# Two heads' last state columns in one matrix product, and the state's increment in two column halves, in an mLSTM cell followed by a gated feed-forward block

## The chip, the core and the metric

The kernel runs on one core of a Trainium2 chip. The metric is the device time of one execution in microseconds (us). The core has a matrix engine (PE, whose weight loads are listed apart as PEld), a vector engine (DVE), an activation engine (ACT), a general engine (POOL), and a queue that starts the transfers (SP). Each works through its own instructions in order and waits on semaphores that the others raise.

## What is computed

An mLSTM cell runs over 768 steps for 4 batch rows and 8 heads of 40 dimensions, and its output goes through a feed-forward block with a cosine gate.

```python
for t in range(S):
    m_new = np.maximum(f_gate[:, :, t] + m, i_gate[:, :, t])
    f_stab = np.exp(f_gate[:, :, t] + m - m_new)
    i_stab = np.exp(i_gate[:, :, t] - m_new)
    m = m_new
    C = f_stab * C + i_stab * np.einsum('bhd,bhe->bhde', vt, kt)
    n = f_stab * n + i_stab * kt
    h_tilde = np.einsum('bhde,bhe->bhd', C, qt)
    denom = np.maximum(np.abs(np.einsum('bhd,bhd->bh', n, qt)[:, :, None]), 1.0)
    y[:, :, t] = sigmoid(o_gate[:, :, t]) * h_tilde / denom
x = y.transpose(0, 2, 1, 3).reshape(3072, 320)
h = x @ w_in            # 320 x 2048
out = (h * np.cos(h)) @ w_out
```

## The kernel before

The 768 steps are cut into 6 chunks `c` of 128. A *cell* `n = 4 * c + b` is one chunk of one batch row with all 8 heads, so there are 24 cells. Inside a cell the recurrence becomes matrix products over 128 steps. Heads 2p and 2p+1 form pair `p`; the key dimensions of the even head lie in partitions 0 to 39, those of the odd head in partitions 64 to 103.

A cell goes through these functions:

- `scores(n)` (L450): keys times queries for each head, the two heads of a pair in the two halves of PE's rows. `weigh(n)` (L456) multiplies by the decay `E`.
- `values(n)`: for n >= 4 the tile `vt` is filled, turned, with 32 output partitions for each of four heads. Four head groups are worked one after another. Each has four products of `vs` (values) with `E` (L474) and four products of the state `st` with the decayed queries (L477), each four on the four 32-column strips of PE. Groups 0 and 1 are dimensions 0 to 31 of heads 0 to 3 and of heads 4 to 7. The third plane `vt[:, 2]` takes the last eight dimensions and the normalizer of all heads. It is filled in two groups: heads 4 to 7 with 32 columns (dimensions 16 to 47, of which only the upper half is kept), then heads 0 to 3 with 16 columns over the lower half.
- `normalize_turned(n)`: DVE divides and gates (L486 to L497), POOL writes two thirds of `xT`, the input of the feed-forward block (L496). `normalize(n)` does this for the first four cells.
- `fade(n)`: POOL multiplies the state by its decay (L529), one operation for each half of the partitions, on 40 partitions by 192 elements.
- `seam(n)`: PE turns the last plane into `px` (L542; for the first four cells L537, and L539 in two 64-column halves), and for n < 20 it computes the state's increment `pu` (L547): one product for each pair of heads, 104 weight columns (both heads' weighed keys) by 96 moving columns (both heads' values). Of this product only the two blocks of a head with itself are used.
- `seam_out(n)`: ACT copies `px` to `xT` (L554). `state(n)` adds `pu` to `st`: two DVE additions of 40 x 192 (L566), or two ACT copies in the first four cells (L564).
- `weigh_k(n)` (POOL, L394) weighs the keys for the increment, and `scale_q(n)` (POOL, L432) decays the queries.

`st[b]` has a place of 48 columns for each head. A head's numbers lie in its own 40 partitions, and the rest of its columns are zero, so a product over all 128 partitions takes one head of the pair.

Every product here is in float32. The trace lists two weight loads and two matmuls for each one, two *passes*, so a count of x8 is four products.

Around the cells runs the feed-forward block, in the hand-written order of `both_parts(c, b)`. It works chunk `c` of the block while cell `n = 4(c+1)+b` is computed. Each cell has two halves, `i = 0` and `i = 1`. PE's order is:

- `i = 0`: up products of this half (`pup`, L583 and L586), `scores(n)`, the down products of the half before (`po`, L615), `values(n)`;
- `i = 1`: up products, `seam(n)`, down products.

In each half ACT rounds the up products (L591), DVE subtracts (L594), ACT takes a sine (L599) and DVE multiplies (L603); in `i = 1` the additions of `state(n)` stand on DVE between L594 and L603. The up products have two buffers, which L603 frees for the next half.

The first four cells are written out by hand in `first_cells`. While cells 4 to 7 run, the weights of the feed-forward block come in as 64-bit floats and are converted piece by piece (`to_float32`, L143 to L151, on ACT, DVE and POOL). All big loads are issued on SP's queue in program order. `load_o(c)` (L300) brings the output gates of a chunk in four transfers, one for each block of 32 partitions; `load_two` (L330, L335) brings queries, keys and values two cells at a time, keys and values only after the `seam` that last read their buffer.

Of the kernel before, what the change touches and what calls it, by code (L numbers as in the profile page):

```python
# [29 lines left out]
def kernel(  # L30
# [63 lines left out]
    nc.gpsimd.affine_select(out=wall, in_=wall, compare_op=OP.is_ge, fill=1.0e30, base=0,  # L94
                            pattern=[[0, HP], [1, C]], channel_multiplier=-1)
    ident_b = const.tile([128, 128], BF, name="ident_b")
    pick = const.tile([128, 2, 2, HP, 8], FP, name="pick")
    for e in range(2):
        nc.gpsimd.tensor_copy(out=pick[:, e], in_=ident.rearrange("q (a g i) -> q g a i", a=HP, g=2)[:, :, :, 0:8])


    DV = 48
# [2 lines left out]
    for i in range(2):  # L105
        nc.gpsimd.memset(ks2[i][:, :, :, D:64], 0.0)
        nc.gpsimd.memset(vs2[i][:, :, :, D:DV], 1.0)

    WR = 2 * HP * (C // 32) * D
# [2 lines left out]
        nc.gpsimd.memset(t[:, WR:WR + 32], 0.0)  # L114


    st = [const.tile([128, H, DV], FP, name=f"st{b}") for b in range(B)]
    for t in st:
        nc.gpsimd.memset(t, 0.0)
    og = const.tile([128, B, 3 * C // 32, 32], FP, name="og")  # L120
# [39 lines left out]

    def weights_in(f):
        for i in range(NK):
            src = [(slice(32 * a, 32 * a + 32), w_in_bits[D * (HP * i + a):D * (HP * i + a) + 32, ts(f, WP)]) for a in range(HP)]
            yield w_in_sb[:, i, ts(f, WP)], bits_in(WP, src, pb, WP)
        src = w_last.rearrange("r (a e n two) -> r e a n two", e=2, n=128, two=2)

        yield (w_in_l[:, ts(f, 2)].rearrange("p a n -> p (a n)"),
               bits_in(256, [(slice(64 * e, 64 * e + 64), src[:, e, ts(f, 2)]) for e in range(2)], pb, WP))
# [119 lines left out]
    def vs(n):  # L288
        return vs2[n // 2 % 2][:, n % 2]

    def load_o(c, bs=range(B)):
        if c == 0:
            sig[c] = og.rearrange("q b k i -> q (b k i)")[:, 0:B * DM].rearrange("q (b h d) -> q b h d", b=B, h=H)
            for b in bs:
                nc.sync.dma_start(out=sig[c][:, b], in_=o_gate[b, :, ts(c, C)].rearrange("h t d -> t h d"))
            return
        raw_o[c] = p1.tile([128, B, 2 * C // 32, D], FP, name="o", tag="o")
        src = o_gate.rearrange("b (g a) (c t k) d -> a c t (b g) (k d)", g=2, k=C // 32, t=32)
        for a in range(HP):
            nc.sync.dma_start(out=raw_o[c][32 * a:32 * a + 32].rearrange("t b (g k) d -> t (b g) (k d)", g=2), in_=src[a, c])  # L300

    def sigmoid(c, bs=slice(0, B)):
        if c == 0:
# [87 lines left out]
    def weigh_k(n):  # L391
        if n < N - B:
            kw = p2.tile([128, H, 64], FP, name="kw", tag="kw")
            nc.gpsimd.tensor_tensor(out=kw, in0=ks(n), in1=cols(n, 1, 64), op=OP.mult)  # L394
            kws[n] = kw

    def psum(n):

        return (ps_o, "o") if n < B and n % 2 == 1 else (ps_a, "a")

    def pair(t, p):
        return t[:, 2 * p:2 * p + 2].rearrange("p j d -> p (j d)")[:, 0:PR]
# [27 lines left out]
    def scale_q(n):  # L430
        qG = p1.tile([128, HP, C], FP, name="qG", tag="qG")
        nc.gpsimd.tensor_tensor(out=qG, in0=qkT[n][0], in1=Gs[n], op=OP.mult)  # L432
        Gs[n] = qG
# [24 lines left out]
    def values(n):  # L458
        pool, tag = psum(n)
        E = Es[n]  # L460
        if n < B:
            ph = pool.tile([128, H, D1], FP, name="ph", tag=tag)
            for j in range(2):
                for p in range(HP):
                    h = 2 * p + j
                    nc.tensor.matmul(ph[:, h], E[:, h], vs(n)[:, h, 0:D1], start=True, stop=True)  # L466
            heads_of[n] = ph
            return
        vt = pool.tile([128, 3, C], FP, name="vt", tag=tag)
        state = st[n % B]  # L470
        for i, g, lo, hi in ((0, 0, 0, 32), (1, 1, 0, 32), (2, 1, 16, 48), (2, 0, 32, 48)):
            for a in range(HP):
                h = HP * g + a
                nc.tensor.matmul(vt[32 * a:32 * a + hi - lo, i], vs(n)[:, h, lo:hi], E[:, h], start=True, stop=False)  # L474
            for a in range(HP):
                h = HP * g + a
                nc.tensor.matmul(vt[32 * a:32 * a + hi - lo, i], state[:, h, lo:hi], Gs[n][:, h // 2], start=False, stop=True)  # L477
        heads_of[n] = vt

    FROM0, FROM1 = 8, 24  # L480
# [19 lines left out]
    def normalize(n):  # L500
        c, b = divmod(n, B)
        hs = heads_of[n]
        dn = p2.tile([128, H], FP, name="dn", tag="dn")

        nc.vector.scalar_tensor_tensor(out=dn, in0=hs[:, :, D], scalar=-TWO_PI, in1=least, op0=OP.mult, op1=OP.max)
        nc.vector.scalar_tensor_tensor(out=dn, in0=hs[:, :, D], scalar=TWO_PI, in1=dn, op0=OP.mult, op1=OP.max)
        nc.vector.reciprocal(out=dn, in_=dn)
        y = p1.tile([128, 3 * C], FP, name="y", tag="yt")[:, 0:DM]
        t = p1.tile([128, 3 * C], FP, name="yo", tag="db")[:, 0:DM].rearrange("q (h d) -> q h d", h=H)
        nc.vector.tensor_tensor(out=t, in0=sig[c][:, b], in1=hs[:, :, 0:D], op=OP.mult)  # L510
        for lo, hi, x in ((0, 32, 0), (32, D, KL)):
            nc.vector.tensor_tensor(out=y[:, x:x + H * (hi - lo)].rearrange("q (h d) -> q h d", h=H), in0=t[:, :, lo:hi],
                                    in1=dn.unsqueeze(2).to_broadcast([128, H, hi - lo]), op=OP.mult)
        ys[n] = y

    ys, pus, pxs = {}, {}, {}
# [1 line left out]
    def halves(n):  # L518
        for j in range(2):
            r = slice(64 * j, 64 * j + D)  # L520
            yield j, r, st[n % B].rearrange("q (p j) d -> q p j d", j=2)[r, :, j]

    def fade(n):

        if B <= n < N - B:
            c, b = divmod(n, B)
            for j, r, s in halves(n):
                d = tab[r, c, 3, ts(b, H)].rearrange("p (a j) -> p a j", j=2)[:, :, j]
                nc.gpsimd.tensor_tensor(out=s, in0=s, in1=d.unsqueeze(2).to_broadcast([D, HP, DV]), op=OP.mult)  # L529

    def seam(n):

        pool, tag = psum(n)
        if n < B:
            px = pool.tile([128, NK + 1, C], FP, name="px", tag=tag)
            for i in range(NK):
                nc.tensor.transpose(px[:, i], ys[n][:, ts(i, 128)], ident)  # L537
            for e in range(2):
                nc.tensor.matmul(px[64 * e:64 * e + 64, NK], ys[n][:, KL:DM], ident, start=True, stop=True)  # L539
        else:  # L540
            px = pool.tile([128, C], FP, name="px", tag=tag)
            nc.tensor.matmul(px, pick.rearrange("q e g a i -> q (e g a i)"), ys[n][:, 2], start=True, stop=True)  # L542
        pxs[n] = px
        if n < N - B:
            pu = pool.tile([128, HP, 2, DV], FP, name="pu", tag=tag)
            for p in range(HP):
                nc.tensor.matmul(pu[0:PR, p].rearrange("p j d -> p (j d)"), pair(kws[n], p),  # L547
                                 vs(n)[:, 2 * p:2 * p + 2].rearrange("p j d -> p (j d)"), start=True, stop=True)
            pus[n] = pu

    def seam_out(n):
# [7 lines left out]

    def state(n):  # L560
        if n < N - B:
            for j, r, s in halves(n):
                if n < B:
                    nc.scalar.copy(out=s, in_=pus[n][r, :, j])  # L564
                else:
                    nc.vector.tensor_tensor(out=s, in0=s, in1=pus[n][r, :, j], op=OP.add)  # L566


    gs, po = {}, {}
# [59 lines left out]
    def first_cells():  # L629
# [107 lines left out]
        load_E(B + 2)  # L737
        decay(B)
        weigh_k(B)
        scale_q(B)  # L740
        for f in range(2, NF // 4):
            last_rows(f)
# [14 lines left out]
    def both_parts(c, b):  # L757
# [3 lines left out]
        for i in range(2):  # L761
# [15 lines left out]
            if i == 0:  # L777
                if cell:
                    weigh(n)
                    if n + 1 < N:  # L780
                        decay_exponents(n + 1)
                for e in range(2):
                    up.sin(e)
                    up.gate(e)
                if b == 0 and c + 1 < NC:
                    sigmoid(c + 1)

                if c == 0 and b > 0 and pieces:
                    to_float32(*pieces.pop(0))
                if cell and n + 1 < N and (c > 0 or b > 0):  # L790
                    decay(n + 1)
            else:
                if cell:
                    seam_out(n)
                if pieces:
                    to_float32(*pieces.pop(0))
                if cell:
                    state(n)
                for e in range(2):
                    up.sin(e)  # L800
                    up.gate(e)
                while pieces:
                    to_float32(*pieces.pop(0))
                if cell and n + 1 < N:
                    weigh_k(n + 1)
            if f2 > 0:
                down(c, f2 - 1)
            elif c > 0:
                down(c - 1, NF // 2 - 1)
# [62 lines left out]
```

## Time and profile before

| What | Value |
|---|---|
| time, median of 3 runs | 587.3 us (586.58 to 589.53) |
| span of the profiled execution | 586.8 us |
| mean granted PE clock | 0.968 |
| one cell from 8 to 19, in the chain | 21.95 us |
| one cell from 20 to 23, in the chain | 21.2 us |
| HBM read, written | 54.07 MB, 5.16 MB |

Of the profiled execution the span is listed and no further time; it lies between the fastest run and the median.

The profile lists each engine's busy time, groups of instructions by source line, and the chain of work that ended last: at each step, what released the step, or the instruction before it on its engine. A row of a group gives the busy time of all its instructions, the mean duration of one in ns, and the idle time of the engine just before them. Matmuls overlap in time, so the mean duration of one is longer than what it adds to PE's time; what it adds is read from the chain, where each piece runs to the start of the next.

### The profile page before, as it was taken

The numbers are of one execution on the slowest core, as the hardware profiler recorded it, in microseconds if no ns is written. First come the engines' busy times: TensorE is split into PE (matmuls) and PEld (weight loads), VectorE is DVE, ScalarE is ACT, GpSimd is POOL, SyncE is SP. The second block draws the span as 40 slices with busy tenths as digits, with TensorE's granted clock in tenths as the row PEclk, the third lists the DMA queues.
The fourth block names the chain that finished last, engine by engine and source line by source line (L and its number), as shares of the span: only waits on it lengthen the run. The fifth ranks groups of instructions, "written<-read, shape, count | busy, mean of one in ns | idle before, by whom it ended". The sixth has DMA issues, their size and how long they took to land.

```text
span 586.8 us, 8874 instructions
## 1 busy us (share of the span) xinstructions
PE 562.0 (96%) x3404; PEld 336.7 (57%) x3404; DVE 361.6 (62%) x677; ACT 257.2 (44%) x411; POOL 140.7 (24%) x170
## 2 busy tenths in 40 slices
PE   8997869888999999999999999999999999999997
PEld 5874435454556556556556556566556566555454
DVE  5665997787666666666666666666666575423131
ACT  4857617184264343373343373343374251233222
POOL 6524354343321221221221221221211110000000
PEclk9858979897999999999999999999999999999999
DMA  9999999974814914914824714914910000010001
GB/s 142 226 232 208 229 245 234 202 167 89 153 47 90 167 32 91 153 46 91 155 44 90 143 55 89 173 26 91 153 45 1 1 2 1 0 45 1 0 1 45
DMA packets 125546, 58.76 MB, mean 100 GB/s; under 512 B 61328, under 2 KB 121824, under 8 KB 125504
## 3 DMA queue, kind: packets, MB, share of 16 engines
q1 hardware_dynamic: 125360, 58.00, 51.2%
q8 instruction: 27, 0.44, 0.4%
q0 software_dynamic: 96, 0.18, 0.1%
q14 instruction: 15, 0.12, 0.1%
q10 hardware_dynamic: 48, 0.02, 0.0%
HBM read 54.07 MB, written 5.16 MB: 101 GB/s over the span
## 4 chain that ended last, share of the span: by engine, by line
PE 82%; DMA 9%; DVE 3%; SPq 3%; POOL 2%; issue 1%; ACT 0%; DVEq 0%; ACTq 0%; POOLq 0%
PE po L615 32%; PE pup L583 26%; PE pup L586 8%; PE ps L450 4%; PE vt L474 3%; DMA bits<-in_moe_w_in_dram 3%; PE vt L477 3%; PE pu L547 2%; DMA vs<-in_v_dram 2%; PE ph L466 1%; DMA G<-G_d 1%; PE px L542 1%; DMA kr<-in_k_dram 1%; SPq L335 1%; DMA o<-in_o_gate_dram 1%; DMA qr<-in_q_dram 1%
## 5 line engine op out<-in xcount | busy, mean ns | idle before, releaser
L615 PE MATMUL po<-w_out_sb,g 128*128 128x320 f32 x768 | 222.6, 444 | 1.8 <-POOL w_out_sb L151 1.8
L615 PEld LDWEIGHTS po<-w_out_sb,g 128*128 128x128 f32 x768 | 145.0, 194 | 66.0 <-issue 10.1
L583 PE MATMUL pup<-xT,w_in_sb 128*128 128x512 f32 x384 | 176.7, 603 | 0.8 <-DVE g L603 0.7
L594 DVE SCALAR_TENSOR_TENSOR n<-pup,n 128x512 f32<-128x512 f32 x96 | 61.7, 684 | 159.4 <-ACT n L591 159.4
L591 ACT ACTIVATE n<-pup 128x512 int32<-128x512 f32 x96 | 51.9, 592 | 238.0 <-PE pup L586 237.9
L583 PEld LDWEIGHTS pup<-xT,w_in_sb 128*128 128x128 f32 x384 | 71.7, 192 | 80.2 <-issue 67.9
L599 ACT ACTIVATE n<-n 128x512 f32<-128x512 f32 x96 | 58.8, 630 | 18.6 <-DVE n L594 16.6
L603 DVE SCALAR_TENSOR_TENSOR g<-pup,n 128x512 f32<-128x512 f32 x96 | 61.6, 683 | 1.7
L381 POOL TENSOR_SCALAR_AFFINE_SELECT E<-E 128x1024 f32<-128x1024 f32 x22 | 24.0, 1091 | 133.7 <-DVE E L380 133.7
L586 PE MATMUL pup<-xT,w_in_l 64*128 64x512 f32 x192 | 54.2, 641 | 0.0
L432 POOL TENSOR_TENSOR qG<-t,G 128x512 f32<-128x512 f32 x20 | 25.4, 1271 | 69.6 <-DVE t L423 64.2
L450 PEld LDWEIGHTS ps<-t,t 40*128 40x128 f32 x384 | 26.6, 200 | 21.5 <-issue 21.2
L450 PE MATMUL ps<-t,t 40*128 40x128 f32 x384 | 28.2, 289 | 10.8 <-DVE t L423 10.8
L474 PE MATMUL vt<-E,vs 128*32 128x128 f32 (+1 forms) x640 | 33.7, 283 | 4.3 <-DMA vs<-in_v_dram 4.3
L496 POOL TENSOR_TENSOR xT<-yt,db 128x256 f32<-128x256 f32 x20 | 14.5, 724 | 96.7 <-DVE db L493 96.7
L389 ACT ACTIVATE E<-E 128x1024 f32<-128x1024 f32 x24 | 25.4, 1058 | 26.7 <-POOL E L381 25.4
L586 PEld LDWEIGHTS pup<-xT,w_in_l 64*128 64x128 f32 x192 | 14.4, 184 | 36.4 <-issue 34.9
L477 PE MATMUL vt<-qG,st 128*32 128x128 f32 (+1 forms) x640 | 33.3, 280 | 0.0
L456 DVE TENSOR_TENSOR E<-ps,E 128x512 f32<-128x512 f32 x48 | 30.7, 679 | 2.6 <-PE ps L450 2.6
L389 ACT ACT_TABLE_LOAD x21 | 26.9, 1283 | 0.4
L380 DVE TENSOR_TENSOR E<-E,tab 128x1024 f32<-128x1024 f32 x22 | 26.7, 1214 | 0.0
L474 PEld LDWEIGHTS vt<-E,vs 128*32 128x32 f32 (+1 forms) x640 | 17.9, 109 | 13.1 <-DVE g L603 6.6
(134 smaller groups left out, 518.2 us busy)
## 6 DMA issues: line engine op xcount, KB each, us to landing
E<-M_d SPq DMA_DIRECT2D x10, 1024.0 KB, 6.0
qr<-in_q_dram SPq DMA_DIRECT2D x40, 160.0 KB, 3.8
kr<-in_k_dram SPq DMA_DIRECT2D x40, 160.0 KB, 4.9
G<-G_d SPq DMA_DIRECT2D x20, 256.0 KB, 6.9
bits<-in_moe_w_out_dram SPq DMA_DIRECT2D x8, 640.0 KB, 6.3
bits<-in_moe_w_in_dram SPq DMA_DIRECT2D x32, 128.0 KB, 4.3
out_dram<-o_sb SPq DMA_DIRECT2D x24, 160.0 KB, 1.8
o<-in_o_gate_dram SPq DMA_DIRECT2D x20, 160.0 KB, 6.0
```

What stands on the lines that cost most here:

```text
L389: nc.scalar.activation(out=Es[n], in_=Es[n], func=AF.Exp, scale=-1.0)
L450: nc.tensor.matmul(ps[j][:, p], kT[r, p], qT[r, p], start=True, stop=True)
L456: nc.vector.tensor_tensor(out=w, in0=pss[n][j], in1=w, op=OP.mult)
L474: nc.tensor.matmul(vt[32 * a:32 * a + hi - lo, i], vs(n)[:, h, lo:hi], E[:, h], start=True, stop=False)
L477: nc.tensor.matmul(vt[32 * a:32 * a + hi - lo, i], state[:, h, lo:hi], Gs[n][:, h // 2], start=False, stop=True)
L583: nc.tensor.matmul(pu, w_in_sb[:, i, ts(2 * f2 + e, 128)], x(i), start=(i == 0), stop=False)
L586: nc.tensor.matmul(pu, w_in_l[r, f2], x(NK, r), start=False, stop=True)
L591: nc.scalar.activation(out=self.n[e], in_=self.pu[e], func=AF.Copy, bias=0.25)
L594: nc.vector.scalar_tensor_tensor(out=self.n[e].bitcast(FP), in0=self.pu[e], scalar=0.25, in1=self.n[e], op0=OP.add, op1=OP.subtract)
L599: nc.scalar.activation(out=r, in_=r, func=AF.Sin, scale=TWO_PI_DOWN)
L603: nc.vector.scalar_tensor_tensor(out=g, in0=self.pu[e], scalar=TWO_PI, in1=self.n[e].bitcast(FP), op0=OP.mult, op1=OP.mult)
L615: nc.tensor.matmul(po[c][b], gs[c, f][:, ts(b, C)], w_out_sb[:, f], start=(f == 0), stop=(f == NF - 1))
```

## The change

The heads are dealt anew over the planes: plane 0 takes the even heads' first 32 dimensions, plane 1 the odd heads', and plane 2 the last part of both heads of a pair, side by side. The state tile is laid out to match: 4 x 32 columns of even heads, 4 x 32 of odd heads, 4 x 32 in which each pair has 16 columns of the even and 16 of the odd head. So plane 2 needs one state product for a pair in place of two. Its odd heads' values come from a new tile `vr2` with 16 zero columns ahead, which POOL fills for two cells at a time (`odd_values`). The state's increment is computed head by head, with 40 weight columns by 48 moving columns, the even head in PE's lower 64 columns and the odd one in the upper 64. `fade` and `state` follow the state's two pieces: four operations for a cell in place of two. The rows of `w_in`, the output gates and the order of `y` follow the new dealing; `load_o` has eight transfers in place of four.

```diff
-    pick = const.tile([128, 2, 2, HP, 8], FP, name="pick")
+    pick = const.tile([128, 2, HP, 2, 8], FP, name="pick")
...
+    vr2 = [const.tile([128, 2, HP, 32], FP, name=f"vr{i}") for i in range(2)]
+    for t in vr2:
+        nc.gpsimd.memset(t, 0.0)
...
-    st = [const.tile([128, H, DV], FP, name=f"st{b}") for b in range(B)]
+    st = [const.tile([128, 2 * HP * DV], FP, name=f"st{b}") for b in range(B)]
...
-            src = [(slice(32 * a, 32 * a + 32), w_in_bits[D * (HP * i + a):D * (HP * i + a) + 32, ts(f, WP)]) for a in range(HP)]
+            src = [(slice(32 * a, 32 * a + 32), w_in_bits[D * (NK * a + i):D * (NK * a + i) + 32, ts(f, WP)]) for a in range(HP)]
...
-        src = o_gate.rearrange("b (g a) (c t k) d -> a c t (b g) (k d)", g=2, k=C // 32, t=32)
+        src = o_gate.rearrange("b (a g) (c t k) d -> a g c t b (k d)", g=2, k=C // 32, t=32)
         for a in range(HP):
-            nc.sync.dma_start(out=raw_o[c][32 * a:32 * a + 32].rearrange("t b (g k) d -> t (b g) (k d)", g=2), in_=src[a, c])
+            for g in range(2):
+                dst = raw_o[c][32 * a:32 * a + 32].rearrange("t b (g k) d -> t g b (k d)", g=2)[:, g]
+                nc.sync.dma_start(out=dst, in_=src[a, g, c])
...
+    def odd_values(n):
+        if n % 2 == 0:
+            src = vs2[n // 2 % 2].rearrange("q n (a g) d -> q n a g d", g=2)[:, :, :, 1, 32:DV]
+            nc.gpsimd.tensor_copy(out=vr2[n // 2 % 2][:, :, :, 16:32], in_=src)
...
-        for i, g, lo, hi in ((0, 0, 0, 32), (1, 1, 0, 32), (2, 1, 16, 48), (2, 0, 32, 48)):
+        for i in range(3):
+            if i < 2:
+                for a in range(HP):
+                    h = 2 * a + i
+                    nc.tensor.matmul(vt[32 * a:32 * a + 32, i], vs(n)[:, h, 0:32], E[:, h], start=True, stop=False)
+            else:
+                for a in range(HP):
+                    nc.tensor.matmul(vt[32 * a:32 * a + 32, i], vr2[n // 2 % 2][:, n % 2, a], E[:, 2 * a + 1], start=True, stop=False)
+                for a in range(HP):
+                    nc.tensor.matmul(vt[32 * a:32 * a + 16, i], vs(n)[:, 2 * a, 32:DV], E[:, 2 * a], start=False, stop=False)
             for a in range(HP):
-                h = HP * g + a
-                nc.tensor.matmul(vt[32 * a:32 * a + hi - lo, i], vs(n)[:, h, lo:hi], E[:, h], start=True, stop=False)
-            for a in range(HP):
-                h = HP * g + a
-                nc.tensor.matmul(vt[32 * a:32 * a + hi - lo, i], state[:, h, lo:hi], Gs[n][:, h // 2], start=False, stop=True)
+                nc.tensor.matmul(vt[32 * a:32 * a + 32, i], state[:, ts(HP * i + a, 32)], Gs[n][:, a], start=False, stop=True)
...
     def halves(n):
         for j in range(2):
             r = slice(64 * j, 64 * j + D)
-            yield j, r, st[n % B].rearrange("q (p j) d -> q p j d", j=2)[r, :, j]
+            for lo, hi, x in ((0, 32, HP * 32 * j), (32, DV, H * 32)):
+                s = st[n % B][r, x:x + HP * 32].rearrange("q (p d) -> q p d", p=HP)
+                yield j, r, s if lo == 0 else s[:, :, 16 * j:16 * j + 16], slice(lo, hi)
...
-            pu = pool.tile([128, HP, 2, DV], FP, name="pu", tag=tag)
+            pu = pool.tile([128, HP, DV], FP, name="pu", tag=tag)
             for p in range(HP):
-                nc.tensor.matmul(pu[0:PR, p].rearrange("p j d -> p (j d)"), pair(kws[n], p),
-                                 vs(n)[:, 2 * p:2 * p + 2].rearrange("p j d -> p (j d)"), start=True, stop=True)
+                for j in range(2):
+                    h = 2 * p + j
+                    nc.tensor.matmul(pu[64 * j:64 * j + D, p], kws[n][:, h, 0:D], vs(n)[:, h], start=True, stop=True)
...
     def state(n):
         if n < N - B:
-            for j, r, s in halves(n):
+            for j, r, s, w in halves(n):
                 if n < B:
-                    nc.scalar.copy(out=s, in_=pus[n][r, :, j])
+                    nc.scalar.copy(out=s, in_=pus[n][r, :, w])
                 else:
-                    nc.vector.tensor_tensor(out=s, in0=s, in1=pus[n][r, :, j], op=OP.add)
+                    nc.vector.tensor_tensor(out=s, in0=s, in1=pus[n][r, :, w], op=OP.add)
...
         weigh_k(B)
+        odd_values(B)
         scale_q(B)
...
                     weigh_k(n + 1)
+                    odd_values(n + 1)
```

More of the change, by code (lines that the diff above doesn't have):

```diff
@@ L96 @@
     ident_b = const.tile([128, 128], BF, name="ident_b")
-    pick = const.tile([128, 2, 2, HP, 8], FP, name="pick")
+    pick = const.tile([128, 2, HP, 2, 8], FP, name="pick")
     for e in range(2):
-        nc.gpsimd.tensor_copy(out=pick[:, e], in_=ident.rearrange("q (a g i) -> q g a i", a=HP, g=2)[:, :, :, 0:8])
+        nc.gpsimd.tensor_copy(out=pick[:, e], in_=ident.rearrange("q (a g i) -> q a g i", a=HP, g=2)[:, :, :, 0:8])
     DV = 48
@@ L510, in normalize @@
         nc.vector.tensor_tensor(out=t, in0=sig[c][:, b], in1=hs[:, :, 0:D], op=OP.mult)
-        for lo, hi, x in ((0, 32, 0), (32, D, KL)):
-            nc.vector.tensor_tensor(out=y[:, x:x + H * (hi - lo)].rearrange("q (h d) -> q h d", h=H), in0=t[:, :, lo:hi],
-                                    in1=dn.unsqueeze(2).to_broadcast([128, H, hi - lo]), op=OP.mult)
+        for lo, hi, o in ((0, 32, y[:, 0:KL].rearrange("q (g a d) -> q a g d", g=2, a=HP)),
+                          (32, D, y[:, KL:DM].rearrange("q (a g d) -> q a g d", g=2, a=HP))):
+            nc.vector.tensor_tensor(out=o, in0=t[:, :, lo:hi].rearrange("q (a g) d -> q a g d", g=2),
+                                    in1=dn.rearrange("q (a g) -> q a g", g=2).unsqueeze(3).to_broadcast([128, HP, 2, hi - lo]), op=OP.mult)
         ys[n] = y
@@ L526, in fade @@
             c, b = divmod(n, B)
-            for j, r, s in halves(n):
+            for j, r, s, w in halves(n):
                 d = tab[r, c, 3, ts(b, H)].rearrange("p (a j) -> p a j", j=2)[:, :, j]
-                nc.gpsimd.tensor_tensor(out=s, in0=s, in1=d.unsqueeze(2).to_broadcast([D, HP, DV]), op=OP.mult)
+                nc.gpsimd.tensor_tensor(out=s, in0=s, in1=d.unsqueeze(2).to_broadcast([D, HP, w.stop - w.start]), op=OP.mult)
     def seam(n):
@@ L561, in state @@
         if n < N - B:
-            for j, r, s in halves(n):
+            for j, r, s, w in halves(n):
                 if n < B:
-                    nc.scalar.copy(out=s, in_=pus[n][r, :, j])
+                    nc.scalar.copy(out=s, in_=pus[n][r, :, w])
                 else:
-                    nc.vector.tensor_tensor(out=s, in0=s, in1=pus[n][r, :, j], op=OP.add)
+                    nc.vector.tensor_tensor(out=s, in0=s, in1=pus[n][r, :, w], op=OP.add)
     gs, po = {}, {}
```

## The prediction

> **What bounds the kernel now.** I read the page first (busy times, the slices), then the chain of waits, then the timeline of one cell, then single groups.
>
> ```profile
> PE 562.0 (96%) x3404; PEld 336.7 (57%) x3404; DVE 361.6 (62%) x677; ACT 257.2 (44%) x411; POOL 140.7 (24%) x170
> ...
> PEclk9858979897999999999999999999999999999999
> DMA  9999999974814914914824714914910000010001
> ```
>
> PE is busy for 96%. The slices (14.7 us each) show two stages: in the first nine DMA is full and PE's clock dips; after them the clock stays high and DMA has room. The chain of waits of one cell (start, length, line) in the second stage:
>
> ```profile
> 190.91 0.35 PE vt L474 x8
> 191.26 0.22 PE vt L477 x8
> ...
> 192.57 0.22 PE vt L477 x8
> 192.79 3.63 PE pup L583 x8
> 196.42 1.06 PE pup L586 x4
> 197.48 0.42 PE px L542 x2
> 197.90 0.72 PE pu L547 x8
> 198.62 4.33 PE po L615 x16
> 202.96 3.43 PE pup L583 x8
> 206.39 1.06 PE pup L586 x4
> 207.45 0.89 PE ps L450 x16
> 208.34 4.50 PE po L615 x16
> ```
>
> Every piece is PE, end to end, and the cell takes 21.95 us. From cell 8 on (138 us) the end is set by PE's own pieces; what they gain or lose is gained or lost in full while the other engines keep up. The early stage is different. The stretches below give length, then busy time and count of PE, PEld, DVE, ACT, POOL, then clock, DMA share and GB/s:
>
> ```profile
> 38.00:41.00 3.00, 2.68 (x11) 1.09 (x11) 2.45 (x8) 0.00 (x0) 0.00 (x0) 0.50 1.18 276
> 105.00:118.00 13.00, 10.38 (x75) 6.34 (x77) 9.34 (x12) 2.31 (x4) 5.42 (x4) 0.87 1.16 193
> 126.00:138.00 12.00, 9.27 (x31) 4.66 (x29) 11.70 (x20) 5.55 (x10) 6.43 (x6) 1.00 0.16 27
> 170.85:192.80 21.95, 21.95 (x147) 13.19 (x147) 14.23 (x27) 11.18 (x19) 5.14 (x6) 1.00 0.41 91
> ```
>
> DMA is at or over a full share until the last weights have landed, then DVE (11.70 of 12.00 us) converts them, and only then is PE the bound.
>
> **State products.** `vt` goes from eight groups of four products to seven: the odd heads' values (32 columns), the even heads' (16) and one state product of 32 columns for a pair. A group of x8 costs 0.22 us in the chain whether its weight columns are 32 (191.26) or 16 (192.57), since 128 moving columns pace it. So one group less is 0.22 us for each of the cells 8 to 23: 16 x 0.22 = 3.5 us. For cells 4 to 7 (another 0.9) I take nothing, since PE idles there for data; the 0.9 goes into the range.
>
> **The increment.** No row shows 40 x 48 products in column halves, so I bound them. Four products of 104 x 96 cost 0.72 us, 90 ns a pass. The `ph` products (L466: 128 weight columns, 41 moving) take 1.74 us for x16 in the early chain, 109 ns: the weight load paces these. The slope is 19 ns over 24 columns, 0.79 ns each, and 40 columns come to 90 - 64 x 0.79 = 39 ns. By moving columns: four strips side by side pass 128 columns in 0.22 / 2 = 0.11 us, and `po` passes 320 in 4.33 / 16 = 0.271 us, 0.84 ns a column, which makes 48 columns 0.11 - 80 x 0.84 ns = 42 ns. The longer decides: 42 ns.
>
> Do two halves run side by side? The nearest row has just this form, the 64-column halves of `px` in a first cell:
>
> ```profile
> 26.63 0.22 PE px L537 x2
> 26.85 0.37 PE px L539 x4
> 27.22 0.90 PE pu L547 x8
> ```
>
> Four passes of 128 columns one after another would be 0.44 us; they took 0.37 with what it costs to change between full width and halves. That cost is in the chain: the first group of `vt` 0.35 against 0.22 (0.13 to go in); `pu` 0.90 after the halves against 0.72 after a full-width piece, and `po` 4.50 after the row halves of `ps` against 4.33 (0.17 to 0.18 to come out). In `seam` the old `pu` had neither. New: 8 x 0.042 + 0.13 + 0.17 = 0.64 us, against 0.72, a gain of 0.08. With no overlap at all: 16 x 0.042 + 0.30 = 0.97, a loss of 0.25. I take the overlap, by its nearest row L539. Cells 8 to 19: 12 x 0.08 = 1.0 us gained; at the other end 3.0 lost.
>
> The Trainium skill speaks against this part: "TensorEngine Tiling (Array Packing)", section "Instruction Overhead", states some 60 cycles of overhead for each matmul, so that one free column lasts as long as 60, and advises against a tiling factor out of a dimension that is already small. The shortest products of the trace (41 moving columns, `ph`) are paced by their weight loads, so no row shows this. By the rule 48 columns would cost as 60 do, an estimate of 42 + 12 x 0.84 = 52 ns, `pu` would be 0.72, and the gain of this part nothing: 1.0 us less in the sum.
>
> **DVE's four additions.** The groups that show it:
>
> ```profile
> L486 DVE TENSOR_SCALAR dt<-vt 128x128 f32<-128x128 f32 x20 | 5.9, 293 | 24.2 <-PE vt L477 24.2
> L566 DVE TENSOR_TENSOR st<-st,pu 40x192 f32<-40x192 f32 x32 | 11.1, 347 | 0.5
> L529 POOL TENSOR_TENSOR st<-st,tab 40x192 f32<-40x192 f32 x32 | 17.2, 538 | 1.2
> ```
>
> From 192 elements (347 ns) and 128 (293) the slope is 0.84 ns; 128 and 64 elements come to 293 + 239 = 532 ns against 347, twice a cell: 0.37 us more, and at most 0.69 if a piece costs what the whole did. Queued behind are the two gates L603, which PE's next up products wait for. In the timeline:
>
> ```profile
> 243.29 0.72 DVE L566 TENSOR_TENSOR st<-st,pu 40x192 f32<-40x192 f32 x2
> 244.04 1.29 DVE L603 SCALAR_TENSOR_TENSOR g<-pup,n 128x512 f32<-128x512 f32 x2
> ...
> 246.68 3.60 PE L583 MATMUL pup<-xT,w_in_sb 128*128 128x512 f32 x8
> ```
>
> The gates end at 245.33 and PE needs their buffers at 246.68, so 1.35 us of `po` cover the 0.37. A shorter `pu` moves PE and DVE's start alike. In `i = 0` PE comes 0.22 earlier against a cover of 1.7 (gates to 256.81, up products at 258.54). Nothing in cells 8 to 19. In cell 7 DVE is on the chain (state at 129.28, gates, L583 idle 0.33 for the gate, then the transposes that `ps` waits 2.62 for): +0.37 there.
>
> **POOL, SP, ACT, `normalize`.** `fade` goes to four operations. From 192 elements (538) and 256 (L496, 724) up to 512 (1055 for L394) a piece of 128 is near 440 and one of 64 near 330: +0.46 us a cell, done by 241.6, against the addition at 243.29; uncovered it would be 12 x 0.46 = 5.5. `odd_values` is a copy of 128 elements, between 236 ns (L99, 64 elements) and 540, each second cell; behind it on POOL stand `scale_q` (246.43) and the mask L381, after idle times of 4.15 and 8 us. For cell 4 it waits for `vs`, with `scale_q(4)` behind it at 54.78, just when `vs` has landed: +0.3, in the stage that DMA sets. `load_o` adds four issues of 0.46 us (L300's median): 1.8 us of SP ahead of `bits`, `ks` and `vs` at 43.4 to 51.9. DMA is over full just then, so queued transfers cover them; later `load_o`s have idle SP behind them (121.8 to 137.2). Two `vr2` memsets of 256 elements, some 0.3 us each, stand in POOL's opening chain (0.6). Against these in the first cells, `pu` follows halves already, and four increments fall from 0.90 to 1.64 us to about 0.5 to 0.9, 2 us less of PE, and ACT's copies grow by 0.3 us a cell beside it. Until 138 us, after DMA and DVE, I take +0.3 in all, with ends of -2.9 (2 us of `pu`, 0.9 of `vt`) and +3.9 (1.8 SP, 0.6 POOL, 1.5 DVE over cells 4 to 7). The rewritten `normalize` and `w_in` rows keep their counts and sizes: nothing.
>
> **The sum.** -3.5 (state products) - 1.0 (increment) + 0.3 (until 138 us) = -4.2 us on a span of 586.8. The span lies 0.5 under the median, so I carry the change over: 587.3 - 4.2 = 583.1 us.
>
> **Rivals.**
> - *The halves do not overlap.* `pu` 0.97: +3.0 in place of -1.0, so 587.3 - 3.5 + 3.0 + 0.3 = 587.1. For it: no product this small in the trace, and twice the passes. Against it: L539, and the four strips of `vt`.
> - *Each small pass costs what a big one does, one after another* (the side of slower). Place: L547. 16 x 90 ns + 0.30 = 1.74 us, +1.02 for each of 12 cells, 12.2 us, so 587.3 - 3.5 + 12.2 + 0.3 = 596.3. It turns slower than before where `pu` costs over 0.72 + 3.2 / 12 = 0.99 us. Against it: the pace follows the columns in all rows (90 at 104, 109 at 128).
> - *The early stage takes it back.* The 3.9 us above in place of 0.3: 586.7. For it: PE idle 4.33 us for `vs` at 55.97, SP hardly idle, and the clock, which the stretch 138 to 145 shows at 0.52 after PE idled. Against it: DMA is full, and these engines wait for it.
> - *The early stage gains too.* -2.9 in place of 0.3: 587.3 - 3.5 - 1.0 - 2.9 = 579.9.
>
> **How the numbers follow.** A change under 0.5% (2.9 us) can't be told from none here. The forecast has 0.53, with its own range of 581.5 to 584.8: 0.49 of it is faster and 0.04 within. The early gain 0.11 (faster), no overlap 0.13 and the early loss 0.16 (both within), the costly passes 0.07 (slower). So faster 0.60, same 0.33, slower 0.07. The range runs from 580.2 to 587.7: it leaves out the costly passes and most of the early gain.
>
> **What would show it.** The chain of a late cell should have seven groups of `vt` with 1.66 us in place of 1.88, `pu` near 0.64 for x16 with `po` after it at 4.50, and the two at 21.65 us for the cell (was 21.95). L566 should be x64 with a mean near 265 ns, and L583 no wait for L603. `pu` over 0.99, or a wait of PE for DVE or POOL after 150 us, would make me wrong; cell 8's `ps` (138.23) coming later than 139 would show the early loss.

## The result, and the profile after

The changed kernel takes 584.48 us (median of 17 runs, 580.64 to 586.71); the kernel before, in runs beside it, 587.91 us (585.36 to 591.43). The ratio is 0.993, with a 95% interval of 0.9909 to 0.9952: 4.1 us less by the ratio (3.4 by the two medians), uncertain by 1.3, against 4.2 predicted. The profiled execution has a span of 582.6 us and took 584.48, so 1.9 us lie around the span. The span of 586.8 before thus belongs to an execution of about 588.7 us, a little over its median; the prediction carried the difference alone, so this does not touch it.

The chain of waits in a first cell and in the same late cell as before (start, length, line):

```profile
22.04 0.37 PE px L560 x4
22.41 0.34 PE pu L570 x16
...
190.45 0.36 PE vt L488 x8
190.80 0.22 PE vt L495 x8
191.02 0.22 PE vt L488 x8
191.24 0.22 PE vt L495 x8
191.46 0.22 PE vt L491 x8
191.68 0.22 PE vt L493 x8
191.89 0.22 PE vt L495 x8
192.11 3.63 PE pup L605 x8
195.74 1.06 PE pup L608 x4
196.80 0.42 PE px L563 x2
197.22 0.47 PE pu L570 x16
197.69 4.50 PE po L637 x16
...
212.09 0.36 PE vt L488 x8
```

`vt` is seven groups, 1.66 us where it was 1.88. `pu` with twice the passes is 0.47 us where it was 0.72, and `po` after it 4.50 where it was 4.33: the price of leaving the halves stands on the next piece. In the first cell, where `pu` follows `px` in halves already, it takes 0.34 us: the passes alone. From `vt` to `vt` the cell takes 212.09 - 190.45 = 21.64 us; before it was 212.85 - 190.91 = 21.94. All of it is still PE, so cells 8 to 19 give 12 x 0.30 us and cells 20 to 23, which have no increment, 4 x 0.22: 4.5 us from cell 8 on. From the `vt` of cell 8 to the end of the span it is 435.4 us where it was 439.8.

The groups of instructions (shape and count, then busy us and mean ns of one):

```profile
L550 POOL TENSOR_TENSOR st<-st,tab 40x128 f32<-40x128 f32 x32 | 13.9, 434 | 1.2
L550 POOL TENSOR_TENSOR st<-st,tab 40x64 f32<-40x64 f32 x32 | 11.4, 356 | 0.0
L570 PE MATMUL pu<-vs,kw 128*40 128x48 f32 x320 | 11.4, 217 | 0.0
L588 DVE TENSOR_TENSOR st<-st,pu 40x128 f32<-40x128 f32 x32 | 9.0, 281 | 0.5
L588 DVE TENSOR_TENSOR st<-st,pu 40x64 f32<-40x64 f32 x32 | 6.8, 214 | 0.0
```

DVE and POOL work in smaller pieces, as estimated (281 and 214 ns against 293 and 239; 434 and 356 against 440 and 330). They cost less than the sum of their lengths, since neighbours overlap: in the timeline the four additions of a cell take 0.86 us where two took 0.72.

The early stage in stretches of time (length; busy time and count of PE, PEld, DVE, ACT, POOL; clock, DMA share, GB/s):

```profile
105.00:118.00 13.00, 10.79 (x91) 6.50 (x93) 10.60 (x14) 2.31 (x4) 5.57 (x4) 1.00 1.14 197
118.00:126.00 8.00, 5.86 (x47) 2.54 (x38) 6.35 (x17) 7.20 (x12) 2.96 (x5) 1.00 1.07 266
126.00:138.00 12.00, 9.44 (x38) 4.77 (x32) 11.70 (x21) 5.80 (x11) 7.34 (x8) 1.00 0.14 27
138.00:145.00 7.00, 6.59 (x25) 4.82 (x26) 5.80 (x9) 3.39 (x4) 2.35 (x3) 0.51 1.01 187
```

It still runs after DMA, then after DVE (11.70 of 12.00 us again), and PE takes over at the same place: in these two profiled executions cell 8's `ps` starts at 138.41, it was 138.23.

### The profile page after: what moved, and what is told of

The parts are those of the page before. It is cut to its first block, busy times and chain, and to the rows that moved or that the text cites. A ratio compares the mean times of both kernels' runs of the same rounds, so it can differ in the third digit from the quotient of the medians.

```text
span 582.6 us, 8973 instructions
## 1 busy us (share of the span) xinstructions
PE 553.2 (95%) x3404; PEld 325.7 (56%) x3404; DVE 362.9 (62%) x709; ACT 257.1 (44%) x419; POOL 150.4 (26%) x214
## 4 chain that ended last, share of the span: by engine, by line
PE 85%; DVE 5%; DMA 5%; SPq 2%; POOL 2%; issue 1%; ACT 0%; POOLq 0%; DVEq 0%; ACTq 0%
PE po L637 35%; PE pup L605 27%; PE pup L608 8%; PE ps L462 4%; PE vt L495 2%; PE vt L488 2%; DMA E<-M_d 2%; DMA o<-in_o_gate_dram 1%; PE px L563 1%; PE pu L570 1%; DMA ks<-in_k_dram 1%; SPq L140 1%; PE ph L478 1%; PE pt L425 1%; DVE w_out_sb L153 1%
## 5 line engine op out<-in xcount | busy, mean ns | idle before, releaser
L613 ACT ACTIVATE n<-pup 128x512 int32<-128x512 f32 x96 | 51.9, 592 | 235.6 <-PE pup L608 235.6
L396 ACT ACT_TABLE_LOAD x21 | 26.9, 1283 | 0.4
L495 PE MATMUL vt<-qG,st 128*32 128x128 f32 x480 | 24.9, 280 | 0.8 <-POOL qG L444 0.8
L550 POOL TENSOR_TENSOR st<-st,tab 40x128 f32<-40x128 f32 x64 | 24.1, 395 | 1.2
```

The source lines that it names most:

```text
L396: nc.scalar.activation(out=Es[n], in_=Es[n], func=AF.Exp, scale=-1.0)
L495: nc.tensor.matmul(vt[32 * a:32 * a + 32, i], state[:, ts(HP * i + a, 32)], Gs[n][:, a], start=False, stop=True)
L613: nc.scalar.activation(out=self.n[e], in_=self.pu[e], func=AF.Copy, bias=0.25)
```

## The experiments

Eleven kernels, in three groups that each ran beside the kernel before. For each I read two numbers: the length of a late cell from the chain, which is the same to 0.01 us in all cells of a kind, and the time against the kernel before. What is left between them belongs to the part before cell 8's `vt`, which starts near 147 us, or to chance in the times. e4 and e7, with one time each, are not in the table.

| Kernel | Cell 8 to 19, 20 to 23 (us) | From cell 8 on | Ratio (95% interval) | In us | Left for the early stage |
|---|---|---|---|---|---|
| before | 21.94, 21.19 | 0 | 1 | 0 | 0 |
| changed | 21.64, 20.97 | -4.5 | 0.993 (0.9909 to 0.9952) | -4.1 | +0.4 |
| e1 `vt` alone | 21.72, 20.97 | -3.5 | 0.9993 (0.997 to 1.0017) | -0.4 | +3.1 |
| e2 `pu` alone | 21.86, 21.19 | -1.0 | 0.9986 (0.9957 to 1.0016) | -0.8 | +0.2 |
| e3 `pu` ahead of `px` | 21.44, 20.97 | -6.9 | 0.9899 (0.9876 to 0.9923) | -5.9 | +1.0 |
| e5 `load_o` later | 21.64, 20.97 | -4.5 | 0.9918 (0.989 to 0.9946) | -4.8 | -0.3 |
| e6 `odd_values` behind | 21.64, 20.97 | -4.5 | 0.9925 (0.9895 to 0.9955) | -4.4 | +0.1 |
| e8 all three | 21.44, 20.97 | -6.9 | 0.9891 (0.9861 to 0.9921) | -6.4 | +0.5 |
| e9 halves in cells 0 to 3 alone | 21.72, 20.97 | -3.5 | 0.9969 (0.9944 to 0.9993) | -1.8 | +1.7 |
| e10 halves from cell 4 on | 21.64, 20.97 | -4.5 | 0.9974 (0.9953 to 0.9996) | -1.5 | +3.0 |
| e11 `pu` ahead, `load_o` later | 21.44, 20.97 | -6.9 | 0.9899 (0.9864 to 0.9934) | -5.9 | +1.0 |

The fourth column is the ratio less 1, times 587 us. The last one is uncertain by some 1.5 us, as the intervals are.

**e1, the state products alone.** The increment goes back to pairs.

```diff
-            pu = pool.tile([128, HP, DV], FP, name="pu", tag=tag)
+            pu = pool.tile([128, HP, 2, DV], FP, name="pu", tag=tag)
             for p in range(HP):
-                for j in range(2):
-                    h = 2 * p + j
-                    nc.tensor.matmul(pu[64 * j:64 * j + D, p], kws[n][:, h, 0:D], vs(n)[:, h], start=True, stop=True)
+                nc.tensor.matmul(pu[0:PR, p].rearrange("p j d -> p (j d)"), pair(kws[n], p),
+                                 vs(n)[:, 2 * p:2 * p + 2].rearrange("p j d -> p (j d)"), start=True, stop=True)
```

> The new dealing and the merged state product, but the increment as before (one product of 104 x 96 for a pair). Theory (two separate gains on PE's path, 3.5 us of state products and 1.0 us of increment): vt has seven groups, pu is back at 0.72 us and po after it at 4.33; about 1.0 us slower than the changed kernel, 3.2 us faster than the kernel before. Rival (the halves bring nothing): as fast as the changed kernel within 0.3 us.

Its chain has `pu` and `po` as expected:

```profile
199.49 0.72 PE pu L568 x8
200.21 4.33 PE po L636 x16
```

The late cells gained 0.22 us each, but the time only 0.4 us. The late half of the theory holds, and the total does not: 3 us, uncertain by 1.4, went in the early stage. e9 and e10 ask for them.

**e2, the increment alone**, in the kernel before: the same edit the other way round.

> The kernel before with one edit: the increment head by head in column halves, and state adds from it with two operations as before. Theory: pu about 0.47 us for x16, po after it 4.50, a gain of 0.08 us in each of cells 8 to 19, so 1.0 us faster than the kernel before, vt unchanged with eight groups. Rival (the early stage, where four increments fall from 0.90 to 0.34 us, is worth more): over 2 us faster. Rival (nothing): within 0.3 us.

`pu` is 0.47 and `po` 4.50, the late cell 21.86: the 0.08 us a cell is there. The time (0.8 us less, interval from 2.5 less to 0.9 more) agrees and cannot tell it from nothing. The four increments of the first cells gained nothing by themselves.

**e3, the increment ahead of the turned plane.**

```diff
-            px = pool.tile([128, C], FP, name="px", tag=tag)
-            nc.tensor.matmul(px, pick..., ys[n][:, 2], start=True, stop=True)
...
+            increment(n, pool, tag)
+            px = pool.tile([128, C], FP, name="px", tag=tag)
+            nc.tensor.matmul(px, pick..., ys[n][:, 2], start=True, stop=True)
```

> The changed kernel with the increment ahead of the turned plane px from cell 4 on, so that PE goes from row halves to column halves to full width, one change of its division less. Theory (a change of division costs 0.13 to 0.20 us wherever it stands): px, pu and po together fall from 5.39 us to 5.20 to 5.27 in cells 8 to 19, 1.4 to 2.3 us faster than the changed kernel; ACT's copy of px comes about 0.5 us later, which nobody waits for. Rival (the cost belongs to the first product of a kind, or px is waited for): no gain, or slower.

The chain of waits of its late cell:

```profile
197.20 0.47 PE pu L558 x16
197.67 0.42 PE px L575 x2
198.09 4.31 PE po L642 x16
202.40 3.43 PE pup L610 x8
```

In the changed kernel the three pieces are 0.42 + 0.47 + 4.50 = 5.39 us, here 5.20. PE goes from the row halves of L613 straight to column halves, which costs what going from full width cost, and `px` then pays for leaving them, as it paid before for leaving the row halves. One change out of three is gone: 0.20 us in each of 12 cells. The theory holds. The time is 0.9899 of the kernel before; the interval lies under that of the changed kernel's ratio but for an overlap of 0.0014, so that this kernel beats the changed one is read from the chain, and the times agree with it.

**e4, the two halves in turn.** The loops over `p` and `j` change places, so that four even heads come before four odd ones.

> The changed kernel with the order of the increment's eight products turned: four even heads (lower columns) first, then four odd heads (upper columns). If two halves overlap only where neighbours in the program alternate: pu 16 x 0.042 + 0.13 = 0.80 us, 0.33 more for each of 12 cells, 4 us slower than the changed kernel. If PE takes later products of a free half ahead: pu stays at 0.47 and the time does not change.

`pu` took 0.67 us in the chain, between the two, and the late cell 21.84; the one time was 583.65 us, too near to the changed kernel's to add to this. The matmuls of `pu` in three stretches of one cell (time, then busy us and count of PE and PEld):

```profile
194.10:194.31 0.21, 0.20 (x5) 0.20 (x6) 0.00 (x0) 0.00 (x0) 1.00 1.24 193
194.31:194.47 0.16, 0.16 (x11) 0.16 (x9) 0.00 (x0) 0.00 (x0) 1.00 1.15 176
194.47:194.69 0.22, 0.22 (x13) 0.22 (x7) 0.00 (x0) 0.00 (x0) 1.00 1.28 191
```

A matmul counts in each stretch that it reaches into. In the first 0.21 us five passes of the lower half start alone, one each 42 ns or so. Then the upper half starts beside them, ahead of the lower half's last three, and runs on alone at the end. (The view does not name the half; this is read from the pace.) So PE does take products of a free half ahead, and the opening's "in order" is not strict for PE, but it does not reach far enough to hide this order. With neighbours alternating, as in the change, both halves run from the start.

**e5, e6 and e8, three costs of the early stage.** In the changed kernel's timeline (start, length, engine and line; in brackets how long the engine sat idle before, and for what) SP's queue is held by the first `load_o`, and cell 4 waits for its values:

```profile
40.09 6.44 SPq L307 DMA_DIRECT2D o<-in_o_gate_dram  x8
46.70 0.39 SPq L178 DMA_DIRECT2D bits<-in_moe_w_out_dram  x1
47.19 0.42 SPq L342 DMA_DIRECT2D ks<-in_k_dram  x1
47.70 3.69 SPq L342 DMA_DIRECT2D vs<-in_v_dram  x1
...
56.98 0.29 POOL L407 COPY vr<-vs 128x128 f32<-128x128 f32 x1 [1.59 <-DMA vs<-in_v_dram]
...
57.06 0.65 PE L488 MATMUL vt<-E,vs 128*32 128x128 f32 x8 [6.84 <-DMA vs<-in_v_dram]
57.22 1.26 POOL L444 TENSOR_TENSOR qG<-t,G 128x512 f32<-128x512 f32 x1
...
58.54 0.66 PE L495 MATMUL vt<-qG,st 128*32 128x128 f32 x8 [0.83 <-POOL qG L444]
```

The same places in the kernel before:

```profile
40.47 2.18 SPq L300 DMA_DIRECT2D o<-in_o_gate_dram  x4
...
45.52 6.36 SPq L335 DMA_DIRECT2D vs<-in_v_dram  x1
...
55.97 0.66 PE L474 MATMUL vt<-E,vs 128*32 128x128 f32 x8 [4.33 <-DMA vs<-in_v_dram]
```

`vs` is issued 2.2 us later and cell 4's `vt` starts 1.1 us later. PE waits 6.84 us for `vs` (4.33 before, but PE also came 1.4 us sooner now), and 0.83 for `scale_q`, which stands behind the copy that waits for `vs` too. SP's long hold has only moved from `vs` (6.36 us) to `load_o` (6.44): SP is past both at 51.4 us, before at 51.9. e5 moves the load, e6 the copy; e8 does both, takes the `vr2` memsets out of POOL's opening chain, and has e3's order.

```diff
-        load_o(1)
         outs.append((0, weights_out(0)))
...
         load_two(B, "Kv")
+        load_o(1)
```

```diff
-        odd_values(B)
         scale_q(B)
+        odd_values(B)
...
```

> The changed kernel with the first load_o (now eight transfers, 6.4 us of SP's time at 40.1 us) issued behind the keys and values of cell 4. Theory (it is the doubled transfers on SP that make vs late): vs is issued near 44 us and lands near 55 in place of 57, the vt of cell 4 starts 1.5 to 2 us earlier; if that lasts to 138 us the time falls by 1 to 2 us, if the weights' DMA sets the early stage anyway it does not move.

> The changed kernel with odd_values behind scale_q in POOL's order, in both places. Theory (for cell 4 the copy that waits for vs holds back scale_q, and PE waits 0.83 us for it): the products of the state follow at once after those of E, cell 4 is 0.8 to 1.5 us earlier; nothing in cells 8 to 23, where both have time. Rival (the early stage is set by DMA): the time does not move.

> The changed kernel with the increment ahead of px, the first load_o behind the keys and values of cell 4, odd_values behind scale_q, and the two vr2 memsets out of POOL's opening chain (0.5 us). Theory (the late part of e3 and the early losses add): cells 8 to 19 at 21.44 us as with the increment ahead of px alone, PE's first transposes 0.5 us earlier, cell 4 some 2 us earlier; 1 to 3 us faster than with the increment ahead alone, 6 to 9 us faster than the kernel before. Rival (DMA and the clock set the early stage): as fast as with the increment ahead alone.

In e5 `vs` is issued at 41.55 and cell 4's `vt` starts at 53.50 in place of 57.06, in its profile:

```profile
41.03 0.41 SPq L342 DMA_DIRECT2D ks<-in_k_dram  x1
41.55 6.77 SPq L342 DMA_DIRECT2D vs<-in_v_dram  x1
48.37 5.33 SPq L307 DMA_DIRECT2D o<-in_o_gate_dram  x8
```

So the load ahead of `vs` is what holds it back; as e5 moves the whole load, which stood there in the kernel before too, it does not show what the doubling alone costs. Of the 3.6 us, 0.2 are left when cell 8's `ps` starts in that profile (138.25 against 138.41). Its `vt` starts 1.6 us earlier (145.61 against 147.17), but by the clock: from 138.02 to 144.84 us it was 0.75 in e5's profile and 0.50 in the changed kernel's, and `ps` took 1.16 us in place of 2.08. The time (0.9918) cannot be told from the changed kernel's 0.993. e6 moved nothing (0.9925): in its profile the copy stands at 58.40 behind `scale_q`, and PE waits 0.57 for `scale_q` still, as the keys that POOL weighs ahead of it came late there. e8 (0.9891) is as fast as e3, within their intervals: the rival, that DMA and the clock set the early stage, is not refuted, though the intervals leave room for most of the 1 to 3 us of the theory. e11 has the load and e3's order alone:

> The changed kernel with the increment ahead of px and the first load_o behind the keys and values of cell 4, and nothing else moved. Theory (late gain 2.4 us, 12 x 0.20, and the early 1.5 us that the load alone gave in its profile): 3 to 4 us faster than the changed kernel, near 580.5. Rival (the early stage gives it back): 2.4 us faster, as with the increment ahead alone.

It gave 580.75 us, 0.9899, e3's ratio: 1.8 us under the changed kernel by the ratios, uncertain by 2.4. That is nearer the rival's 2.4 than the theory's 3 to 4, and decides nothing; the "early 1.5 us" that the theory added was the clock of e5's profile.

**e7, the cover of the additions.** Each of the four additions runs five times, so the state is no longer the reference's.

> The changed kernel with each of the four additions of the increment done five times (the state is then not the reference's). Sixteen additions more cost 16 x 0.215 = 3.4 us of DVE in cells 4 to 19. If the cover is the 1.35 us of the prediction (last gate to the next up products), PE waits about 2.1 us in each of cells 8 to 19, 25 us in all; if each of the two buffers counts by itself (the first gate ends 1.75 us before its buffer is needed), about 1.7 us, 20 us in all. If DVE is not covered at all: 41 us.

It took 645.72 us, 58 us over the median of the kernel before in that group (587.49) and so about 62 over the changed kernel, and all three numbers were too low. PE waited for the gates 16 times, 49.0 us in all. PE's busy time and clock around one wait (columns as in the stretches above):

```profile
290.00:294.60 4.60, 4.60 (x24) 2.96 (x18) 3.85 (x13) 2.27 (x5) 0.48 (x1) 1.00 0.02 4
294.60:297.90 3.30, 0.07 (x2) 0.03 (x1) 3.00 (x12) 0.00 (x0) 0.00 (x0) 1.00 0.00 0
297.90:303.20 5.30, 5.30 (x9) 2.00 (x9) 2.44 (x3) 0.00 (x0) 1.27 (x1) 0.68 0.53 117
```

And its timeline in two cells:

```profile
266.46 5.43 DVE L589 TENSOR_TENSOR st<-st,pu 40x128 f32<-40x128 f32 x20
271.93 1.29 DVE L626 SCALAR_TENSOR_TENSOR g<-pup,n 128x512 f32<-128x512 f32 x2
272.76 3.67 PE L606 MATMUL pup<-xT,w_in_sb 128*128 128x512 f32 x8 [2.84 <-DVE g L626]
...
297.87 5.40 PE L606 MATMUL pup<-xT,w_in_sb 128*128 128x512 f32 x8 [3.23 <-DVE g L626]
```

Two things came on top. Additions to the same tile run one after another and no longer overlap: twenty take 5.43 us, 4.6 more than the change's four (0.86), not 3.4. And after some of the waits the clock falls: after the 3.23 us the next stretch has 0.68, and `pup` takes 5.40 us. Of the twelve waits of cells 8 to 19 (2.74 to 3.23 us) seven were followed by a `pup` of 5.37 to 5.40 us and five by one of 3.67 to 3.70. The length of the wait does not sort them: one of 2.74 us is among the seven, one of 3.22 among the five.

What does sort them is how a wait lies in time. The seven falls begin at 195.76, 223.07, 298.16, 325.47, 376.67, 427.87 and 479.07 us, whole multiples of 3.41 us apart, and each lasts 3.41 us. Cut into such steps, the trace shows PE busy for 0.29 to 1.41 us in the step ahead of each fall, and for 1.50 us or more in every step around the other five waits. The two cases nearest each other, after waits of 2.74 and 2.84 us, each a step and the next:

```profile
219.65:223.07 3.42, 1.41 (x4) 0.69 (x5) 3.25 (x10) 0.00 (x0) 0.00 (x0) 1.00 1.26 198
223.07:226.48 3.41, 3.41 (x6) 1.29 (x4) 1.07 (x2) 0.00 (x0) 1.27 (x1) 0.50 0.18 30
...
270.85:274.27 3.42, 1.50 (x4) 0.82 (x5) 3.25 (x9) 0.00 (x0) 0.00 (x0) 1.00 0.20 26
274.27:277.68 3.41, 3.41 (x18) 1.46 (x18) 0.90 (x1) 0.15 (x1) 1.27 (x1) 1.00 0.00 0
```

This is read from one trace, and it does not account for the falls of the early stage, where PE was busy throughout (13.60 of 13.60 us at 0.50 in e1, from 13.3 us).

The cover itself is the one counted buffer by buffer: 4.6 - 1.75 = 2.8 us, where nine of the twelve waits are 2.74 to 2.84 us. So four additions, 0.14 us longer than two, are far inside it.

**e9 and e10, which early cells pay.** The increment in halves in cells 0 to 3 alone, and from cell 4 on alone:

```diff
+            if n >= B:
+                pu = pool.tile([128, HP, 2, DV], FP, name="pu", tag=tag)
...
+            else:
                 pu = pool.tile([128, HP, DV], FP, name="pu", tag=tag)
```

> The changed kernel with the increment in column halves in cells 0 to 3 alone and by pairs from cell 4 on. What is asked: why the vt change alone (increment by pairs everywhere) gained only 0.4 us of the 3.5 that its late cells gained. Theory (the four shorter increments of the first cells, 2 us of PE, pay for what the change costs early): 1.0 us slower than the changed kernel, 2 us or more faster than vt alone. Rival (they are hidden, vt alone was unlucky in its early clock): this kernel equals vt alone where that is measured well, both 3 us faster than the kernel before.

> The complement: the increment by pairs in cells 0 to 3 and in column halves from cell 4 on. Late cells at 21.64 us as in the changed kernel. Theory (first cells pay): 2 us slower than the changed kernel. Rival (hidden): equal to the changed kernel within 0.5 us.

e10 has the changed kernel's late cells to the hundredth and is 2.6 us slower by the ratios (each uncertain by 1.3, the difference by 1.8); it lacks only the short increments of the first four cells. Like e1, the other kernel with pairs there, it loses 3 us early. The six kernels that have the halves in all cells and the new dealing lose -0.3 to 1.0. e9 lies between, at 1.7: 1.4 us faster than e1, uncertain by 2.0. So the times suggest that the first cells' increments are worth some 2 us in the new dealing, as the theory has it, but the profiles do not show it. In e10's profile cell 8's `ps` starts at 138.09 us, no later than in the changed kernel's (138.41), though in e1's it starts at 141.96. Over the profiles of all kernels but e7 it starts anywhere between 136.4 (e4) and 142.0, a scatter wider than the effect: e3 and e6, with short increments in all cells, have 140.66 and 140.78.

## Why the prediction was right, step by step

- **What bounds the kernel.** Right. Every late piece is PE's own, and the change of a late cell is the change of its PE pieces, in all kernels but e7. The slices were read a little off: DMA has eight full digits and then a 7, and the clock's tenth digit is a 7 too, from the half clock at the start of cell 8.
- **State products, -3.5 us.** Right: 0.22 us for each of 16 cells, alone in e1 and together with the rest.
- **The increment, -1.0 us.** Right, term by term: 8 x 0.042 = 0.34 us for the passes, 0.13 to go in and 0.17 to come out, 0.64 in all against 0.72. The first-cell `pu`, which follows halves already, shows the passes alone at 0.34. The two rivals of this part fall: e4 shows what less overlap costs (0.67 in place of 0.47), and a lone pass takes 42 ns, not 90. The rule weighed there, of the Trainium skill's page "TensorEngine Tiling (Array Packing)", section "Instruction Overhead", would have made a pass 52 ns by the estimate in the prediction. The measurement decides: 42 ns for 48 columns, 0.88 ns a column, where 128 and 320 take 0.85, so no least length shows here.
- **DVE's additions, nothing late and +0.37 in cell 7.** The cover was right and mis-sized on the safe side: 1.75 us for the first gate, not 1.35, since each buffer frees by itself. The size was too large: 0.14 us a cell, not 0.37, because neighbouring additions overlap. I had added the lengths of single ones.
- **POOL.** `fade` grew by 0.29 us (1.43 for four against 1.14 for two), not 0.46, for the same reason, and nothing late waits for it.
- **The early stage, +0.3 us.** The sum came out (+0.4, by difference, uncertain by 1.3), but not its parts, so that the total was met to 0.1 us is partly luck. I priced the doubled `load_o` at 1.8 us of SP and let the queued transfers cover it. SP was held 6.4 us by it, but as long by `vs` before; `vs` was issued 2.2 us later, and with the wait for `scale_q` the first state products of cell 4 came 2.2 us later (58.54 against 56.36). At cell 8 0.2 us of this are left in the profiles (138.41 against 138.23). The first cells' shorter increments, which I had also seen (2 us) and called hidden, may have paid for it: e1 and e10, without them, have +3 by their times. e10's profile does not bear it out, and it stays open.
- **The rivals.** The costly passes and the missing overlap are ruled out by the chain. The early loss was there in part, 2.2 us at cell 4 in the profile; what took it back before cell 8 is not shown.

What stays open: how an early gain or loss reaches cell 8. e2 has the short increments and no doubled loads, and gained nothing early (0.2 more, uncertain by 1.7). In e1's profile PE is already 5 us behind the changed kernel's when cell 0's increment starts (27.1 against 22.2 us), though PE's program is the same up to there: the clock was 0.50 from 13.3 to 26.9 us, and in the changed kernel's profile only from 18.6 to 22.0. So two executions can lie 5 us apart at this place by the clock alone. Runs of one kernel lie up to 8 us apart; in e1 the longer ones have the lower mean clock (0.946 at 589.8 us, 0.971 at 583.5), in other kernels this is weak or absent (e2: 0.967 at both 590.1 and 584.1 us). One thing runs through all of them: averaged over its runs, every kernel of the table with the new dealing has a mean clock of 0.959 to 0.966, while e2 has 0.968 and the kernel before 0.970 to 0.973 in the three groups. Where this lower clock comes from was not tried; it is as low in the changed kernel as in e1 (0.961 both), so it does not tell these two apart, but it may be part of what the new dealing loses early. Whether pairs in the first cells make a low clock likelier later on was not tried, and the +3 of e1 and e10 rests on medians of 12 runs each.

## What to carry to other kernels

Where one engine is the chain, price an edit in the chain, piece by piece and with the piece that follows: the increment's gain of 0.25 us is visible at once, and 0.17 of it is paid by the next piece. Changes between full width, row halves and column halves of PE cost 0.13 to 0.20 us each, so order the pieces to have few of them: e3, which only swaps two neighbours, gained half as much again as the change. Where DMA is full, splitting a transfer can make the queue that issues it stand there in place of further on, and what lies behind is issued later: here `vs` by 2.2 us, its first user by 1.1. And an early delay read at one place is not an early delay of the kernel: of the 2.2 us at cell 4, 0.2 were left at cell 8.

## What was not expected of the hardware

- Eight transfers of 80 KB held SP for 6.4 us (5.3 in e5, 7.8 in e1) while DMA was full, where four of 160 KB with the same bytes took 2.2 to 2.5 us. Yet from the start of `load_o` to the end of the issue of `vs` SP took 11.3 us with eight (11.8 in e1) and 11.4 with four (11.9 in e2).
- PE works on the second column half ahead of the program's order, but only after five passes of the first half had started alone (0.21 us, e4).
- In e7 waits of PE of 2.74 to 3.23 us cost 1.7 us more or nothing (`pup` 5.40 or 3.70), by how much of a step of 3.41 us they left PE busy: 1.41 us and less lowered the clock of the next step, 1.50 and more did not. The Trainium skill, "TensorE: Matmul & The Clock Gate", section "Why this matters for your kernels", tells to keep idle gaps of PE under about 3 us; in this trace that did not do, since five of the nine gaps of 2.74 to 2.84 us were followed by the lower clock.
